# Empty rows of the expert buckets: stored behind the counts instead of over the whole range in batch 0

## The chip, the cores and the metric

The kernel runs on one core of one Trainium2 chip, as one launch. The metric is the device time in microseconds (us), the median of several runs. Five engines work side by side, each in its own order: TensorE (PE, its weight loads PEld), VectorE (DVE), ScalarE (ACT), GpSimd (POOL) and SyncE (SP), which here issues most of the DMAs.

## The reference

A ReLU-squared attention without softmax is multiplied into u, and its result goes token by token through one of 16 experts. B = 8 batches of S = 1856 tokens, D = 256, z has 64 columns, an expert's hidden width is 1024:

```python
scores = (1.0 / S) * np.matmul(z, z.transpose(0, 2, 1))
attn = np.maximum(scores, 0.0) ** 2
x = (u * np.matmul(attn, v)).reshape(B * S, D)
g_idx = np.argmax(x @ w_group, axis=1)
...
e_idx = np.argmax(xg @ w_expert[g], axis=1)
...
h = np.maximum(xg[mask_e] @ w1[g, e], 0.0)
ye = h @ w2[g, e]
out[tok_idx] = combined[:, None] * ye
```

`combined` is the product of the two softmax weights of the chosen group and expert. Each of the 14848 tokens thus goes to exactly one of 16 experts, and how many an expert gets is known only when the router has run.

## The kernel before, in words

**Attention.** The 8 batches are cut into 4 chunks of queries (512, 512, 512 and 320 wide in batches 1 to 7, 512, 512, 416 and 416 in batch 0), and each chunk into 15 steps of 128 keys: 480 steps `s`, in step with which everything else is issued. `scores` runs six steps ahead of `attn_v`. Each factor is split in a high and a low part, and three products are added. The scores are symmetric, so some tiles are transposed by DVE (`put_mirror`), stored in DRAM (`sym`) and loaded again by `load_mirror` (tile `at`, L326) some steps before they are needed.

**Router.** At the end of a chunk (`chunk_end`) DVE makes `xT` = o * u (L429), ACT splits it (`xh`, L435) and writes planes of 16 bits (`pl`, L464); DMA transposes on SP's queue turn those planes into token rows (`rows`, L470) and the logits into `lgx` (L493). The generators of `route` then take small DVE steps, a few per attention step: the chosen expert, the place of each token in its bucket (`di`, from the running counts `base`), the weight. At the end POOL scatters the rows into the bucket with indirect DMAs (L642).

**Bucket.** `bucket` lies in DRAM and has a region of CAPB rows per expert, RW = 264 words (1056 B) a row: 256 of the token, its weight, its number and filling. The experts are then worked off in fixed numbers of rows, the capacities CAPS (1216 for the largest expert down to 832). A region's rows behind its tokens must therefore hold rows without effect: `padrow`, weight 0 and token number N or more, which the final scatter leaves out. Before the change `prefill` writes the first CMAX = 1280 rows of every region with `padrow`, in 32 stores of 640 rows, at steps 1 to 41 of batch 0 (list PFILL), and all scatters come later.

**Experts.** `sort_experts` runs on DVE twice: behind batch 6, when it fixes the two largest experts (NEARLY = 2) for an early start with their first FRZ = 512 rows each, and at the end with the final counts. It writes the experts in order of size to `eli`, and their regions to `rli`; SP reads both into registers (`regs`, L741 and L742). A block of up to 512 rows is then loaded by `load_x`: one DMA transpose (`xp`, L756) and a small load of weights and numbers (`meta`, L759); DVE joins it (`xf`, L770), ACT and DVE split it. `phase1` (L791 to L793) and `phase2_t` (L864) are the expert's two matmuls, ACT and DVE evacuate, `yr` (L877) turns the result back, and POOL scatters it into the output (L889). Expert weights (`raw_e`, L181 and L184) come 4 x 512 KB per expert. Blocks 0 and 1 belong to the two early experts and are worked in among the last steps of batch 7; blocks 2 and 3 are the rest of expert 0 (its place in the order, as everywhere below), 4 and 5 that of expert 1, and then each expert has two or three blocks.

**What sets the order.** In batches 1 to 7 PE, ACT and DVE run in the order in which the code issues them; outside of that a scheduler orders them by its own clock. SP's queue is ordered by the scheduler. SP works strictly in order: while one of its DMAs waits for a semaphore, everything behind it waits too. Its DMAs share eight completion counters. A DMA that touches `bucket` at an address known only at run time counts as touching all of it: it waits for the reads and writes of `bucket` that were issued before.

Two buffers matter below. The planes `pl` and the block loads `xp` share two buffers (`new_pl`), and `rows` has four (`new_rows`):

```python
    def new_pl(name):
        return sb("pl", [P, 2048], U16, 2, name)
```

Of the kernel before, what the change touches and what calls it, by code (L numbers as in the profile page):

```python
# [19 lines left out]
P = 128  # L20
CAPS = (1216, 1136, 1104, 1072, 1024, 1008, 992, 992, 960, 944, 928, 912, 896, 880, 848, 832)
OVT = 256
# [7 lines left out]
def tile_glu_attn_moe(  # L30
# [28 lines left out]
    assert all(sum(x) == S for x in QW)  # L59
    assert all(cv % 16 == 0 and cv >= 2 * P for cv in caps)  # L60
    RW = D + 8
    RU = 2 * RW
    CAPB = (N + 511) // 512 * 512 + 512
    CMAX = (max(caps) + P - 1) // P * P
    NROW = NE * CAPB
    NL = 20
    LP = 48
# [7 lines left out]
    POS = [KB.index(i) for i in range(NQ)]  # L75
    ATL = 7
    NT = 4
    NEARLY = 2
    PFILL = [1 + i for i in range(17)] + [18 + 5 * i // 3 for i in range(2 * NE - 17)]
    assert CMAX % (2 * P) == 0  # L80
    FRZ = min(512, min(caps[:NEARLY]))
    assert min(caps[:NEARLY]) > FRZ or len(set(caps)) == 1

# [5 lines left out]
    def sb(tag, shape, dt, bufs, name):  # L89
        return pool.tile(shape, dt, tag=tag, bufs=bufs, name=name)  # L90
# [28 lines left out]
    def bank(pl, tag, name):  # L119
        return pl.tile([P, 512], F32, tag=tag, name=name)  # L120

    bucket = tc.dram_tile([NROW + OVT, RW], I32, name="bucket")
    views = dram_disjoint_views(bucket, B * NQ * NT)

    padrow = cst("padrow", [P, RW], I32)
# [84 lines left out]
    def new_w():  # L210
        return {"h": [], "l": [], "2": []}
# [135 lines left out]
    def scores(s):  # L347
        b, c, i = steps[s]
        k = key(b, c, i)
        w = QW[b][c]  # L350
        for far in (ATL, 12):
            lb, lc, li = steps[min(s + far, NS - 1)]
            lk = key(lb, lc, li)
            if lk % KT == 0 and mirrored(lb, lc, lk) and ((lc, lk) == (3, 8) and lb < B - 1) == (far != ATL):
                load_mirror(lb, lk // KT, KB[lc])
        if mirrored(b, c, k):
            at = ats[(b, k // KT, KB[c])][:, k % KT]
            ah, al = new_z(f"ah_{s}")[:, 0:w], new_z(f"al_{s}")[:, 0:w]
            nc.scalar.copy(out=ah.rearrange("p (g x) -> p g x", x=32), in_=at)
            nc.vector.tensor_sub(  # L360
                out=al.rearrange("p (g x) -> p g x", x=32), in0=at, in1=f32(ah).rearrange("p (g x) -> p g x", x=32)
            )
            hl[s] = (ah, al)
            return
        z2h, z2l = bz[(b, k // 4)]
        ks = slice((k % 4) * P, (k % 4 + 1) * P)
        zm = zms[(b, c)][:, 0:w]
        ps = bank(ps_s, "s", f"sc_{s}")
        held = pin if s < LEAD + NK else same
        held(nc.tensor.matmul(ps[:, 0:w], z2h[:, ks], zm, start=True, stop=False))  # L370
        held(nc.tensor.matmul(ps[:, 0:w], z2l[:, ks], zm, start=False, stop=True))  # L371
        a = new_zraw(f"r_{s}")[:, 0:w]
        held = pin if s < NK else same
        held(nc.scalar.activation(out=a, in_=ps[:, 0:w], func=AF.Relu, scale=1.0 / S))  # L374
        ah = new_z(f"ah_{s}")[:, 0:w]
        mirror = MB[0] <= b < MB[1] and KB[c] < MC and k // KT < MC and c < POS[k // KT]
        if i in (ACT_TWICE[c] if MB[0] <= b < MB[1] else ()) and s >= NK:
            held(nc.scalar.activation(out=ah, in_=a, func=AF.Square))
            held(nc.scalar.activation(out=a, in_=a, func=AF.Square))
        else:  # L380
            held(nc.scalar.activation(out=a, in_=a, func=AF.Square))  # L381
            held(nc.vector.tensor_copy(out=ah, in_=a))  # L382
        if k < NKF:
            al = new_z(f"al_{s}")[:, 0:w]
            held(nc.vector.tensor_sub(out=al, in0=a, in1=f32(ah)))  # L385
        else:
            al = None
            nc.vector.tensor_sub(out=ah[TAIL:P, :], in0=a[TAIL:P, :], in1=f32(ah[TAIL:P, :]))
        if mirror:
            put_mirror(b, c, k, a)  # L390
        hl[s] = (ah, al)
# [27 lines left out]
    def chunk_end(s):  # L419
# [83 lines left out]
        defer(s + PL + 1, lambda: planes(1))  # L503
        defer(s + LG, logits)
        defer(s + LG + (1 if XO else 0), logits_out)
        wait = 5 if last else 12 if b == 0 and c < 2 else (17 if c == 1 and b < B - 1 else 15) if s + 1 < NS - NK else 8
        alone = b == B - 1 and c >= NQ - 2
        if c % 2 or alone:
            gens.append((max(s + wait, PFILL[-1] + 2), route(b, c // 2, (c % 2,) if alone else (0, 1))))
        if last_sort(b, c):  # L510
            gens.append((0, sort_experts()))
        if last:
# [18 lines left out]
    def route(b, half, hs):  # L531
# [102 lines left out]
        ew = t("ew", [NT8])  # L634
        nc.vector.tensor_reduce(out=ew, in_=sel, axis=AX.X, op=ALU.add)
        yield
        for h, (rows, nt, part) in enumerate(chunks):
            i0 = 4 * h
            nc.vector.tensor_mul(out=rows[:, 0:nt, D].bitcast(F32), in0=ew[:, i0:i0 + nt], in1=smv[:, i0:i0 + nt, 0])
            for i in range(nt):  # L640
                n = part if part and i == nt - 1 else P
                nc.gpsimd.indirect_dma_start(  # L642
                    out=views[(b * NQ + 2 * half + hs[h]) * NT + i],
                    out_offset=bass.IndirectOffsetOnAxis(ap=di[0:n, i0 + i:i0 + i + 1], axis=0),
                    in_=rows[0:n, i, :],
                    in_offset=None,
                )
            yield
# [4 lines left out]
    def sort_experts(final=False):  # L653
# [2 lines left out]


        sq = lambda name: sb("tm", [P, D], F32, 2, name)[:, 0:NE * NE].rearrange("p (a b) -> p a b", b=NE)
        key = cst("skey", [P, NE])
        nc.vector.tensor_sub(out=key, in0=base, in1=ebase)  # L660
        nc.vector.tensor_scalar(out=key, in0=key, scalar1=float(NE), scalar2=None, op0=ALU.mult)
# [31 lines left out]
        t2 = sq("t2")  # L693
        nc.vector.tensor_tensor(out=t2, in0=gt, in1=iota16.unsqueeze(2).to_broadcast([P, NE, NE]), op=ALU.mult)
        yield
        ef = cst("sef", [P, NE])
        nc.vector.tensor_reduce(out=ef, in_=t2.rearrange("p e j -> p j e"), axis=AX.X, op=ALU.add)
        yield
        nc.vector.tensor_copy(out=eli, in_=ef)
# [31 lines left out]
    NB = len(blocks)  # L731
    last_use = {j: max(i for i in range(NB) if blocks[i][0] == j) for j in range(NE)}
    is_sorted = []
    ereg = {}
    rreg = {}

# [164 lines left out]
        ocnt[0] += 1  # L901
        return oviews[ocnt[0] - 1]

    def prefill(i):
        r0, n = i // 2 * CAPB + i % 2 * (CMAX // 2), CMAX // 2
        ins = nc.sync.dma_start(
            bucket[r0:r0 + n, :].rearrange("(p t) w -> p t w", p=P),
            padrow.unsqueeze(1).to_broadcast([P, n // P, RW]),
        )
        tc.keep_in_program_order(ins)  # L910

    nc.vector.memset(warm, 0.0)
    nc.scalar.activation(out=warm, in_=warm, func=AF.Exp)
# [41 lines left out]
    for s in range(NS):  # L955
        b, c, k = steps[s]
        if s == NK:
            region.enter_context(tc.manual_schedule(engines={mybir.EngineType.PE, mybir.EngineType.Activation, mybir.EngineType.DVE}))
        if s == NS - NK:
            region.close()  # L960
        if s in (1, 4):
            pz.pop(0)()
        if s in (2, 6, 9):
            pv.pop(0)()
        if s == 8:
            make_router()
        for i in range(2 * NE):
            if PFILL[i] == s:
                prefill(i)
        nxt = s // NK + 1  # L970
        if k == 3 and nxt < B * NQ:
            load_ut(nxt // NQ, nxt % NQ)
        if b + 1 == B:
            for pc, load, cut in WPREP:
                if (c, k) == load:
                    wts.setdefault(0, new_w())
                    prep[pc] = load_w(regs(0)[0], wts[0], pc, "e0")
                if (c, k) == cut:
                    prep.pop(pc)()
        for what, pb, n in begin.get(s, ()):  # L980
            prep[(what, n)] = (prep_v if what == "v" else prep_z)(pb, n)
        for what, pb, n in split_at.get(s, ()):
            prep.pop((what, n))()
        if k == (5 if s < NK else 5) and nxt < B * NQ:
            prep_zm(nxt // NQ, nxt % NQ)
        if s == NS - NK - 6:
            load_rows(0)
        if s == NS - 6:
            load_rows(1)
        if s == NS - 12:  # L990
            xs.append(join_x(0, rows_b[0][0], blocks[0][2]))
        while ahead < min(NS, s + LEAD + 1, max(4, 3 + s + s // 2)):
            scores(ahead)
            ahead += 1
        attn_v(s)
        if k == NK - 1:
            chunk_end(s)
        run_deferred(s)
        run_gens(s, 2 if b + 1 < B else (3 if c < 3 else 5))
# [3 lines left out]
    def more_rows(i):  # L1003
        if not (deferred or gens):
            while late["loaded"] < min(NB, i + 2):
                load_rows(late["loaded"])
                late["loaded"] += 1

    def early(i):
        run_deferred(late["at"])  # L1010
# [132 lines left out]
    for i, (e, r0, n) in enumerate(blocks):  # L1143
# [10 lines left out]
        def mid(f):  # L1154
            if i < NEARLY:
                early(i)
            elif i > 2 * NEARLY and f % 2 == 0:
                next(planned, None)
            if i + 1 == NB and f > 3 and unsent:
                unsent.pop(0)()  # L1160
            if ld is not None and f in (3, 5):
                sp[(f - 3) // 2]()
# [28 lines left out]
    with tc.For_i(0, kreg) as iv:  # L1191
# [6 lines left out]
        for t in range(2):  # L1198
            nc.gpsimd.indirect_dma_start(
                out=bucket,  # L1200
                out_offset=bass.IndirectOffsetOnAxis(ap=ix[:, t:t + 1], axis=0),
                in_=padrow,
                in_offset=None,
                bounds_check=NROW + OVT - 1,
                oob_is_err=False,
# [43 lines left out]
```

## Time and profile before

| | |
|---|---|
| median of 3 runs | 1456.65 us (1456.34 to 1457.46) |
| the profiled execution's own time | 1457.97 us |
| its span, first to last instruction | 1456.3 us |
| granted clock of PE, mean | 0.997 |
| PE busy | 1438.4 us (99%) |
| DVE, ACT, POOL busy | 1135.6, 920.2, 286.5 us |
| DMA moved | 255.98 MB, 176 GB/s on the mean |
| stores of `padrow` | 32 of 660.0 KB |

How to read it: a row of a timeline has the start and the duration in us, the engine, the line of the kernel, the operation and its tiles, and in brackets how long the engine stood idle before it and what released it. SPq is SP's sequencer: the duration is that of issuing the DMA, not of the transfer. A row of the waits has the waiting engine and line, what it waited for, and us in total, times and the longest. A row of the stretches has the busy time of each engine with its number of instructions, then PE's granted clock, the mean share in which the DMA engines were busy, and GB/s. Matmuls are pipelined, so PE's busy time is not its peak. Batch 0 takes about the first 100 us, batch 7 ends at about 768 us, and the experts fill the time from about 760 us on.

### The profile page before, as it was taken

The numbers are of one execution on the slowest core, as the hardware profiler recorded it, in microseconds if no ns is written. First come the engines' busy times: TensorE is split into PE (matmuls) and PEld (weight loads), VectorE is DVE, ScalarE is ACT, GpSimd is POOL, SyncE is SP. The second block draws the span as 40 slices with busy tenths as digits, with TensorE's granted clock in tenths as the row PEclk, the third lists the DMA queues.
The fourth block names the chain that finished last, engine by engine and source line by source line (L and its number), as shares of the span: only waits on it lengthen the run. The fifth ranks groups of instructions, "written<-read, shape, count | busy, mean of one in ns | idle before, by whom it ended". The sixth has DMA issues, their size and how long they took to land. (4 is left out here: it accounts for less than half of the span.)

```text
span 1456.3 us, 22386 instructions
## 1 busy us (share of the span) xinstructions
PE 1438.4 (99%) x7113; PEld 1240.3 (85%) x7113; DVE 1135.6 (78%) x2338; ACT 920.2 (63%) x1613; POOL 286.5 (20%) x351
## 2 busy tenths in 40 slices
PE   9999999999999999999999999999999999999997
PEld 7898888888888888888788999888888888999986
DVE  7889999999998999989987576776566666666663
ACT  8887887788877878778675344444445444444442
POOL 0002022220222202221114222112211221122122
PEclk9999999999999999999999999999999999999998
DMA  9997979989799797997975464554533554555521
GB/s 290 327 258 210 231 192 259 213 229 217 185 262 217 213 225 188 261 218 176 233 176 150 95 179 86 121 141 123 143 90 96 141 128 130 133 127 133 131 59 44
DMA packets 410808, 255.98 MB, mean 176 GB/s; under 512 B 243791, under 2 KB 370131, under 8 KB 410688
## 3 DMA queue, kind: packets, MB, share of 16 engines
q1 hardware_dynamic: 398864, 223.51, 62.6%
q0 software_dynamic: 11744, 30.90, 6.8%
q8 instruction: 56, 0.92, 0.3%
q14 instruction: 64, 0.52, 0.1%
q10 hardware_dynamic: 80, 0.13, 0.0%
HBM read 108.29 MB, written 89.21 MB: 136 GB/s over the span
## 5 line engine op out<-in xcount | busy, mean ns | idle before, releaser
L407 PE MATMUL o<-ah,vl 128*128 128x512 f32 (+2 forms) x960 | 355.0, 370 | 1.7 <-DVE vl L294 1.5
L408 PE MATMUL o<-ah,vh 128*128 128x512 f32 (+2 forms) x960 | 354.7, 370 | 0.0
L410 PE MATMUL o<-al,vh 128*128 128x512 f32 (+2 forms) x896 | 329.4, 370 | 0.5 <-DVE al L360 0.5
L802 DVE SCALAR_TENSOR_TENSOR hl<-ph,hh 128x512 fp32r<-128x512 f32 (+12 forms) x288 | 173.2, 609 | 149.1 <-ACT hh L796 131.0
L864 PE MATMUL yT<-hh,w_e 128*128 128x512 f32 (+12 forms) x1120 | 269.4, 360 | 0.0
L796 ACT ACTIVATE hh<-ph 128x512 fp32r<-128x512 f32 (+12 forms) x288 | 152.4, 536 | 147.9 <-PE ph L793 140.3
L889 POOL DMA_INDIRECT out_dram<-y,meta x126 | 126.9, 1007 | 493.6 <-DVE y L887 463.1
L864 PEld LDWEIGHTS yT<-hh,w_e 128*128 128x128 f32 x1120 | 200.2, 188 | 25.0
L374 ACT ACTIVATE r<-sc 128x512 f32<-128x512 f32 (+2 forms) x312 | 177.8, 570 | 56.2 <-PE sc L371 38.6
L642 POOL DMA_INDIRECT bucket<-rows,di x121 | 137.5, 1137 | 367.8 <-issue 217.7
L407 PEld LDWEIGHTS o<-ah,vl 128*128 128x128 f32 x960 | 180.4, 188 | 32.1 <-DVE vl L294 2.1
L791 PE MATMUL ph<-xh_m,w1l_e 128*128 128x512 f32 (+12 forms) x576 | 206.8, 361 | 0.8 <-ACT xh_m L775 0.8
L792 PE MATMUL ph<-xh_m,w1h_e 128*128 128x512 f32 (+12 forms) x576 | 207.5, 361 | 0.0
L408 PEld LDWEIGHTS o<-ah,vh 128*128 128x128 f32 x960 | 180.3, 188 | 28.8
L793 PE MATMUL ph<-xl_m,w1h_e 128*128 128x512 f32 (+12 forms) x576 | 203.2, 360 | 0.0
L385 DVE TENSOR_TENSOR al<-r,ah 128x512 fp32r<-128x512 f32 (+2 forms) x280 | 188.0, 672 | 17.0
L410 PEld LDWEIGHTS o<-al,vh 128*128 128x128 f32 x896 | 168.0, 188 | 26.8 <-DVE al L360 0.8
L381 ACT ACTIVATE r<-r 128x512 f32<-128x512 f32 (+2 forms) x284 | 174.0, 613 | 9.0
L864 PE MATMUL yT<-hl,w_e 128*128 128x512 f32 (+12 forms) x560 | 159.2, 360 | 0.0
L867 ACT COPY yp<-yT 128x1024 uint16<-128x1024 uint16 (+2 forms) x70 | 59.2, 848 | 141.9 <-PE yT L864 78.4
L382 DVE CAST ah<-r 128x512 fp32r<-128x512 f32 (+2 forms) x284 | 117.4, 413 | 18.4 <-ACT r L381 13.1
L370 PE MATMUL sc<-zm,z2h 128*128 128x512 f32 (+2 forms) x312 | 120.5, 386 | 1.0 <-ACT r L374 0.6
(166 smaller groups left out, 1967.7 us busy)
## 6 DMA issues: line engine op xcount, KB each, us to landing
raw_e<-in_w_dram SPq DMA_DIRECT2D x64, 512.0 KB
sym<-mt SPq DMA_DIRECT2D x126, 256.0 KB
at<-sym SPq DMA_DIRECT2D x84, 256.0 KB
bucket<-padrow SPq DMA_DIRECT2D x32, 660.0 KB
at<-sym SPq DMA_DIRECT2D x84, 160.0 KB
vr<-in_v_dram SPq DMA_DIRECT2D x24, 512.0 KB
ut<-in_uT_dram SPq DMA_DIRECT2D x23, 512.0 KB
zr<-in_zT_dram SPq DMA_DIRECT2D x47, 128.0 KB
```

Source lines behind the costliest of these rows:

```text
L374: held(nc.scalar.activation(out=a, in_=ps[:, 0:w], func=AF.Relu, scale=1.0 / S))
L381: held(nc.scalar.activation(out=a, in_=a, func=AF.Square))
L385: held(nc.vector.tensor_sub(out=al, in0=a, in1=f32(ah)))
L407: held(nc.tensor.matmul(o, vl[:, dsl], ah, start=(i == 0), stop=False))
L408: held(nc.tensor.matmul(o, vh[:, dsl], ah, start=False, stop=end and al is None))
L410: held(nc.tensor.matmul(o, vh[:, dsl], al, start=False, stop=end))
L791: nc.tensor.matmul(o, wt["l"][d][:, fs], xh[:, d, 0:W], start=(d == 0), stop=False)
L792: nc.tensor.matmul(o, wt["h"][d][:, fs], xh[:, d, 0:W], start=False, stop=False)
L793: nc.tensor.matmul(o, wt["h"][d][:, fs], xl[:, d, 0:W], start=False, stop=(d == ND - 1))
L796: nc.scalar.activation(out=hh[:, 0:W], in_=o, func=AF.Relu)
L802: nc.vector.scalar_tensor_tensor(out=dst, in0=o[:, c0:c1], scalar=0.0, in1=f32(hh[:, c0:c1]), op0=ALU.max, op1=ALU.subtract)
L864: nc.tensor.matmul(o, wt["2"][f // 2][:, w0:w0 + P], hs[f][q // 2][:, 0:n], start=((f, q) == (0, 0)), stop=((f, q) == (NF - 1, 2)))
```

## The change

The prefill goes. Instead the rows behind an expert's tokens are stored once the counts are known, and as many as its capacity. `sort_experts` keeps a copy of the counts (`ends`), SP loads an expert's end into a register, and `pad` stores `padrow` from there. Behind batch 6's sort there are three such stores: 512 rows for expert 0, 512 for expert 1, and another 768 for expert 0. Behind the final counts there is one for each of the experts 1 to 15, of 640 to 1152 rows, ahead of the load of its first block with final counts. A bucket row has 258 words (1032 B) instead of 264. Some small edits come with it: the last mirror loads are issued 11 steps ahead and not 12, the first two chunks of batch 0 are routed as late as those of other batches, the planning of the overflow loop (`plan`) starts at block 9 instead of 5, and `sef` takes the buffer of `srank`.

```diff
+    BW = D + 2
-    CAPB = (N + 511) // 512 * 512 + 512
+    CAPB = N + (max(caps) + P - 1) // P * P
-    PFILL = [1 + i for i in range(17)] + [18 + 5 * i // 3 for i in range(2 * NE - 17)]
-    bucket = tc.dram_tile([NROW + OVT, RW], I32, name="bucket")
+    bucket = tc.dram_tile([NROW + OVT, BW], I32, name="bucket")
-        for far in (ATL, 12):
+        for far in (ATL, 11):
-        wait = 5 if last else 12 if b == 0 and c < 2 else (17 if c == 1 and b < B - 1 else 15) if s + 1 < NS - NK else 8
+        wait = 5 if last else (17 if c == 1 and b < B - 1 else 15) if s + 1 < NS - NK else 8
-                in_=rows[0:n, i, :],
+                in_=rows[0:n, i, 0:BW],
+        ends.append(cst("ends", [P, NE], I32))
+        nc.vector.tensor_copy(out=ends[-1], in_=base)
-    def prefill(i):
-        r0, n = i // 2 * CAPB + i % 2 * (CMAX // 2), CMAX // 2
-        ins = nc.sync.dma_start(
-            bucket[r0:r0 + n, :].rearrange("(p t) w -> p t w", p=P),
-            padrow.unsqueeze(1).to_broadcast([P, n // P, RW]),
-        )
-        tc.keep_in_program_order(ins)
+    def pad(j, n, off=0):
+        if (j, off) in padded:
+            return
+        padded.add((j, off))
+        e = regs(j)[0]
+        r0 = nc.sync.value_load(ends[-1][0:1, ds(e, 1)], min_val=0, max_val=(NE - 1) * CAPB + N)
+        n = (n + P - 1) // P * P
+        nc.sync.dma_start(
+            bucket[ds(r0 + max(off, 0), n), :].rearrange("(p t) w -> p t w", p=P),
+            padrow[:, 0:BW].unsqueeze(1).to_broadcast([P, n // P, BW]),
+        )
+    def pad_for(i):
+        if i < NB:
+            j = blocks[i][0]
+            pad(j, caps[j] - FRZ if j < NEARLY else caps[j], FRZ if j == 0 else -1 if j < NEARLY else 0)
...
+                    if pc == WPREP[0][0]:
+                        pad(0, FRZ)
...
+        if s == NS - NK - 4:
+            pad(1, FRZ)
+        if s == NS - NK + 0:
+            pad(0, caps[0] - FRZ, FRZ)
...
             while late["loaded"] < min(NB, i + 2):
+                pad_for(late["loaded"])
                 load_rows(late["loaded"])
                 late["loaded"] += 1
+            if late["loaded"] >= 2 * NEARLY:
+                pad_for(late["loaded"] + 0)
...
-            elif i > 2 * NEARLY and f % 2 == 0:
+            elif i > 4 * NEARLY and f % 2 == 0:
```

Where the stores stand is seen in SP's queue. The first of three places is the head of batch 7, right behind the loads of the registers for expert 0 (`eli`, `rli`; ISA rows are address arithmetic). Before:

```order
L742 TENSOR_LOAD rli_108
L742 ISA x2
L741 TENSOR_LOAD eli_107
L741 ISA x2
L326 DMA at_7_1_3_9523<-sym_7_1_3_9117 32x10x128 x4
L184 ISA
L184 DMA raw_e0_2_9447<-in_w2_dram 128x4x256
```

And now:

```order
L745 TENSOR_LOAD rli_108
L745 ISA x2
L915 ISA
L915 TENSOR_LOAD ends_9276
L915 ISA x2
L917 ISA
L917 DMA bucket_69<-padrow_70 512x1x258
L325 DMA at_7_1_3_9503<-sym_7_1_3_9085 32x10x128 x4
```

A load of expert 0's end and the first store have moved in ahead of the mirror loads for batch 7's last chunk. Further on in the same queue stands the load of block 0 (`xp_0`), with the logits, rows and mirror loads of batch 7 behind it. Before:

```order
L756 DMA_TRANSPOSE xp_0_9545<-bucket_69 128x4x512
L493 DMA_TRANSPOSE lgx_7_0_9020<-lgp_7_1_9365 128x8x48
L470 DMA_TRANSPOSE rows_7_1_9362<-pl_7_1_9364 128x4x128 x4
L326 DMA at_7_2_3_9604<-sym_7_2_3_9243 32x10x128 x4
L184 ISA
L184 DMA raw_e0_3_9658<-in_w2_dram 128x4x256
L759 ISA
L759 DMA meta_1_9818<-bucket_69 128x4x2
```

And now:

```order
L759 DMA_TRANSPOSE xp_0_9525<-bucket_69 128x4x512
L492 DMA_TRANSPOSE lgx_7_0_8988<-lgp_7_1_9335 128x8x48
L917 ISA
L917 DMA bucket_69<-padrow_70 512x1x258
L469 DMA_TRANSPOSE rows_7_1_9332<-pl_7_1_9334 128x4x128 x4
L325 DMA at_7_2_3_9612<-sym_7_2_3_9211 32x10x128 x4
L917 ISA
L917 DMA bucket_69<-padrow_70 768x1x258
L183 ISA
L183 DMA raw_e0_3_9666<-in_w2_dram 128x4x256
L762 ISA
L762 DMA meta_1_9818<-bucket_69 128x4x2
```

The second store stands between the load of block 0 and the four `rows` transposes of batch 7's second chunk, and the third between the mirror loads and the last weights of expert 0. The second store's wait list names the load `xp_0`, and that of `meta_1` the third store. The third place is expert 2, the first one whose region is stored as a whole, at the load of its first block (`xp_6`). Before:

```order
L756 DMA_TRANSPOSE xp_6_11048<-bucket_69 128x4x512
L181 ISA
L181 DMA raw_e2_0_10756<-in_w1_dram 128x1024
L181 ISA
L181 DMA raw_e2_1_10758<-in_w1_dram 128x1024
```

And now, where the expert's four weight loads are already ahead of it:

```order
L880 DMA_TRANSPOSE yr_3_10675<-yp_3_10674 128x4x128 x3
L917 ISA
L917 DMA bucket_69<-padrow_70 1152x1x258
L745 TENSOR_LOAD rli_108
L745 ISA x2
L915 ISA
L915 TENSOR_LOAD ends_10273
L915 ISA x2
...
L759 ISA
L759 DMA_TRANSPOSE xp_6_11065<-bucket_69 128x4x512
```

The load has moved from ahead of the weights to behind them, behind the turned results of block 3 and behind the store, with eight register loads between the two. On PE, ACT and DVE nothing moves between the head of batch 7 and the final sort but the cast that copies `base` to `ends`.

## Prediction before the run

> **What bounds the kernel now.** I read the page first, then the waits of TensorE (PE), then the stretches by engine.
>
> ```profile
> PE 1438.4 (99%) x7113; PEld 1240.3 (85%) x7113; DVE 1135.6 (78%) x2338; ACT 920.2 (63%) x1613; POOL 286.5 (20%) x351
> ```
>
> PE is busy for 1438.4 of 1456.3 us, and the change takes no matmul away. So it can only move what PE waits. These are its waits, longest first: us in total, times, longest.
>
> ```profile
> PE o L407 <- DVE vl L294: 1.5, 1, 1.5
> ...
> PE pk L605 <- ACT lgp L490: 1.0, 1, 1.0
> PE pl L483 <- DVE xl L440: 0.9, 1, 0.9
> PE ph L791 <- ACT xh_m L775: 0.8, 2, 0.5
> PE sc L370 <- ACT r L374: 0.6, 1, 0.6
> PE o L410 <- DVE al L360: 0.5, 1, 0.5
> ```
>
> All of them together are under 8 us; the rest of PE's idle time is the ends of the span. The pace of the matmuls is no reserve either. The stretches give us, busy time of PE, PEld, DVE, ACT and POOL with their counts, granted clock, DMA share and GB/s:
>
> ```profile
> 0.00:20.00 20.00, 16.79 (x99) 13.58 (x100) 14.29 (x27) 15.62 (x28) 2.69 (x33) 1.00 0.85 245
> ...
> 40.00:60.00 20.00, 20.00 (x90) 16.44 (x89) 16.13 (x30) 16.65 (x27) 0.00 (x0) 1.00 1.09 357
> ...
> 240.00:260.00 20.00, 20.00 (x91) 16.06 (x90) 19.02 (x45) 17.64 (x30) 0.00 (x0) 1.00 1.10 252
> ...
> 1440.00:1460.00 20.00, 5.84 (x32) 4.66 (x30) 2.68 (x7) 1.68 (x4) 6.04 (x6) 0.74 0.11 39
> ```
>
> With the prefill running (40 to 60) PE does 90 matmuls in 20 us, without it (240 to 260) 91. The 32 stores do not slow PE down. An edit that starts from a PE with so few waits has little to win and can lose wherever a wait is new.
>
> **Batch 0: the prefill goes.** Its stores, by their line (ns of one issue, least, median, most):
>
> ```profile
> L906 SPq DMA_DIRECT2D bucket<-padrow x32: 580/1546/2325, 13.2 to 96.8; - x32
> ```
>
> One PE wait lies in their time, at 98.5 us. It goes back to a late transpose of batch 0's logits, which stood among these stores on SP's queue:
>
> ```profile
> 89.84 0.69 DVE L547 COPY lgf<-lgx 128x640 uint16<-128x640 uint16 x1 [1.95 <-DMA lgx<-lgp]
> 92.41 1.04 ACT L435 CAST xh<-xT 128x416 fp32r<-128x416 f32 x2 [1.52 <-DVE xT L429]
> ...
> 99.13 0.46 PE L370 MATMUL sc<-zm,z2h 128*128 128x416 f32 x1 [0.61 <-ACT r L374]
> ```
>
> DVE stood 1.95 us, then ACT 1.52, then PE 0.61. Now nothing stands ahead of that transpose and its route starts five steps later (a wait of 17 instead of 12). I count the 0.6 as won; it lies between 0 and 0.6, since no other PE wait falls in that time.
>
> **The head of batch 7.** This is where the change adds waits. SP's queue there, before:
>
> ```profile
> 734.63 1.84 SPq L326 DMA_DIRECT2D at<-sym  x4
> 736.69 0.43 SPq L184 DMA_DIRECT2D raw_e<-in_w_dram  x1
> ...
> 739.81 5.20 SPq L756 DMA_TRANSPOSE xp<-bucket  x1
> 745.12 1.19 SPq L493 DMA_TRANSPOSE lgx<-lgp  x1
> 746.41 5.15 SPq L470 DMA_TRANSPOSE rows<-pl  x4
> 751.66 2.03 SPq L326 DMA_DIRECT2D at<-sym  x4
> ...
> 760.74 1.80 SPq L493 DMA_TRANSPOSE lgx<-lgp  x1
> ```
>
> The first store stands ahead of the mirror loads at 734.63. It overwrites rows of the bucket, so it waits until batch 6's scatters have landed. When that is, POOL shows: its last scatter, and the iota that reuses a row buffer of those scatters.
>
> ```profile
> 732.06 1.42 POOL L642 DMA_INDIRECT bucket<-rows,di  x1 [0.30 <-issue]
> ...
> 735.65 0.15 POOL L443 IOTA rows<- 128x21 int32 x1 [1.89 <-issue]
> ```
>
> So the store issues at about 735.65; with the shortest issue, 0.58, the mirror loads come at 736.23 instead of 734.63, 1.6 later. Its 512 rows of 1032 B are 0.78 of a prefill store (640 rows of 1056 B). One of those took 1.55 us where they followed one another, 2.33 at most, so the bytes cost between nothing (in a gap of the queue) and 1.8. What stands behind on the same queue, three weight loads and `xp_0`, shifts by 1.6 to 3.4; I take 2.2. The three extra register loads ahead of `xp_0` are hidden, since its issue of 5.20 us is a queue that is full.
>
> The second store is worse. Its address is known only at run time, so it must wait until `xp_0` has read the bucket; and behind it stand the four transposes of `rows_7_1`. How long such a read takes to land is seen at `xp_2`: issued until 803.98, and DVE released at 806.21, 2.2 later.
>
> ```profile
> 802.56 1.42 SPq L756 DMA_TRANSPOSE xp<-bucket  x1
> ...
> 806.21 1.07 DVE L770 COPY xf<-xp 128x1536 uint16<-128x1536 uint16 x1 [3.85 <-DMA xp<-bucket]
> ```
>
> `xp_0`'s issue ended at 745.01; shifted by 2.2 that is 747.2, landed 749.4, the store's issue done 750.0. The `rows` transposes began at 746.41, so they are 3.6 late. For the store's own bytes ahead of them I add 0.4 (between 0 and 1.8): 4.0.
>
> Who waits for them? ACT, then DVE, then PE, with nothing in between:
>
> ```profile
> 752.97 1.05 ACT L464 COPY pl<-xT 128x1024 uint16<-128x1024 uint16 x1 [1.31 <-DMA rows<-pl]
> 753.92 0.61 ACT L435 CAST xh<-xT 128x512 fp32r<-128x512 f32 x1
> ...
> 754.57 0.69 DVE L440 TENSOR_TENSOR xl<-xT,xh 128x512 fp32r<-128x512 f32 x1 [1.33 <-ACT xh L435]
> 755.18 0.53 DVE L547 COPY lgf<-lgx 128x640 uint16<-128x640 uint16 x1
> 755.60 1.35 DVE L770 COPY xf<-xp 128x2048 uint16<-128x2048 uint16 x1
> 756.83 0.32 DVE L552 TENSOR_TENSOR tm<-lgf 128x160 f32<-128x160 f32 x1
> 757.05 0.90 DVE L360 TENSOR_TENSOR al<-at,ah 128x320 fp32r<-128x320 f32 x2
> ...
> 757.61 0.56 PE L410 MATMUL o<-al,vh 128*128 128x320 f32 x2 [0.55 <-DVE al L360]
> ```
>
> ACT may not overwrite the plane buffer until the transposes have read it, and waits 1.31 for that already. Its copies lead to DVE's `xl`, DVE runs without a gap to `al`, and PE waits 0.55 for `al`. The chain has no slack, and ACT's and DVE's order is the same in the changed program there. So PE loses what the transposes lose: **+4.0**, with no cover. Its least is 1.4 (`xp_0` lands at 747.2 as before, plus 0.58, against 746.41); its most is 6.6 (3.4 instead of 2.2 on the queue, and 1.8 for the store's bytes).
>
> Earlier in that stretch ACT also gets its first weight tile 2.2 later, but any PE wait from that lies inside the 4.0: the chain's end is the same.
>
> **The third store** (768 rows, 1.17 of a prefill store, 1.8 us) stands ahead of `meta_1`, which reads the bucket and waits for it to land: 0.58 plus 2.2 to 4.0. So `rows_7_2` and the logits' transpose at 760.74 come 2.8 to 4.6 later than the 4.0, with their landing at about 771 to 772.5. DVE reads them at
>
> ```profile
> 766.47 0.35 DVE L547 COPY lgf<-lgx 128x320 uint16<-128x320 uint16 x1
> ```
>
> and 4.0 later is 770.5. DVE then stands 0 to 2 us. PE is in block 0 there, with several PSUM banks ahead of it, so I take **+0.5** of 0 to 2.
>
> **The per-expert stores.** From expert 1 on, each stands ahead of the `xp` load of its expert, which waits for it to land. The tightest is expert 2's, 1152 rows (1.76 prefill stores, 2.7 us at that pace). `xp_6` moves from ahead of the weights to behind `yr_3` and this store:
>
> ```profile
> 838.39 1.77 SPq L756 DMA_TRANSPOSE xp<-bucket  x1
> ...
> 843.48 4.98 SPq L877 DMA_TRANSPOSE yr<-yp  x3
> ...
> 862.59 1.33 DVE L770 COPY xf<-xp 128x2048 uint16<-128x2048 uint16 x1
> ```
>
> `yr_3` ended at 848.46; plus 0.58, 2.7 and 2.2 for the store, 853.9; plus 1.77 and 2.2 for `xp_6`, 857.9, against its use at 862.59. The cover is 4.7 us, and I count **0**. Without that cover PE would lose microsecond for microsecond. Later experts have a block more of lead. The narrower rows make the scatters 2% smaller, with starts at other offsets:
>
> ```profile
> L642 POOL DMA_INDIRECT bucket<-rows,di x121 | 137.5, 1137 | 367.8 <-issue 217.7
> ```
>
> All but the last three run beside PE's work; for those, which gate `xp_2`, I take 0, between -0.1 and half of the 1.1 us that one takes. The few added DVE casts of 16 columns lie beside PE.
>
> **Sum.** -0.6 + 4.0 + 0.5 = +3.9 us. The profiled execution took 1457.97 us, its span 1456.30 and 1.67 around it; the median of the runs is 1456.65, 1.32 lower. On the median the forecast is 1456.65 + 3.9 = **1460.5 us**, 0.27% slower. A measurement of this kernel can tell about 0.2%, 2.9 us, from no change.
>
> **Rivals.**
> - *The chain catches up.* The stretch in which the first store would issue has some room on the DMA engines (share 0.65):
>
> ```profile
> 720.00:740.00 20.00, 19.12 (x84) 15.06 (x83) 19.29 (x48) 12.09 (x20) 7.82 (x9) 1.00 0.65 179
> ```
>
> If the first store's bytes slip into a gap of the queue, the second costs only its least, 1.4, and with the 0.6 won the sum is +0.8: 1457.5, no change. It decides where the second store ends its issue before 749.2, less than 2.8 behind 746.41. Against it: the 5.20 us of `xp_0`'s issue.
> - *The expert stores block SP.* If a store lands over 4.7 us later than I count, because the 2 MB of weights ahead of it are still under way, `xp_6` is late. At 4 us more than the cover the sum is +7.9: 1464.5. For it: the loads of eight registers stand there too.
> - *The early relief is larger.* The place would be batch 0 and the loads of batch 1: with 32 stores gone, PE would have to win over 2.9 us net, so more than the chain loses. PE's waits before 100 us are 0.6 plus those of the first 10 us, ahead of the first store at 13.2. It would need the chain at its least and 4.3 us won that no row shows: 1453.5.
> - *The clock falls.* PE's longest wait, 1.5 us, lies in the first stretch shown, whose clock is 1.00. After the last matmul the clock falls: in the last stretch PE is busy 5.84 us, and a mean of 0.74 over 20 us is 5.2 us of pulses missing. If it falls to half, that is 10.4 of the 14.2 idle us, so it fell 3.8 us after PE stopped. Should the new stall reach 3.8 us in one piece, and the clock need as long to come back, half of it is lost besides, +1.9: 1462.4. Against it: the stall comes in pieces, at two logits matmuls and then at `al`. [...]
>
> **How the numbers follow.** Forecast, +2.9 to +6.6: 0.50. The chain catches up: 0.28. Expert stores: 0.11. Clock: 0.07. Early relief: 0.04. Slower by over 0.2% is 0.50 + 0.11 + 0.07 = 0.68, within 0.28, faster 0.04. The range runs from 1456.8 (under it the early relief and the lowest part of the first rival) to 1465.0 (over it half of the expert stores' case and little else). The forecast's own range is 1459.6 to 1463.3.
>
> **What would show it.** Right: SP's second store near 749 to 751, `rows` transposes 3 to 5 us late, ACT's `pl` copy waiting about 5 instead of 1.31 for `rows<-pl`, and new PE waits of 3 to 5 us in sum by 763, on `xh`, `xl` or `al`; no PE wait near 98; `xp_6` landed before its `xf`. Wrong: PE without new waits between 735 and 765, or PE waits on `xh_m` in the expert blocks that are longer than the 0.8 of before.

## The result and the profile after

The changed kernel took 1471.66 us (median of 4: 1464.35, 1474.33, 1469.76, 1473.56) against 1456.77 us before; the ratio is 1.0091 [1.0077, 1.0105]. The forecast was 1460.5, between 1456.8 and 1465.0. The direction was right, the loss of 15 us is four times the one forecast. The profiled execution is the fastest of the four (1464.35, span 1462.5); the other three ran at a mean clock of 0.996 where it ran at 0.999.

The waits of TensorE after: us in total, times, longest.

```profile
PE pl L481 <- ACT xh L434: 1.7, 1, 1.7
...
PE yT L867 <- ACT hh L799: 1.3, 1, 1.3
...
PE o L406 <- DVE ah L387: 1.3, 1, 1.3
...
PE o L409 <- DVE al L359: 0.8, 1, 0.8
```

The wait of `sc` on `r` near 98 is gone. New are `pl` on `xh`, `o` on `ah` and a longer `al`, all between 750 and 762. The `yT` on `hh` stands at 805.74: ACT made that `hh` only at 805.09, though the `ph` matmul behind which it stands is drawn until 800.79. No other profile has this wait there, and its cause is open. SP's queue near 740 shows the chain of the prediction:

```profile
733.61 0.69 SPq L917 DMA_DIRECT2D bucket<-padrow  x1
734.41 2.65 SPq L325 DMA_DIRECT2D at<-sym  x4
...
739.55 0.38 SPq L762 DMA_DIRECT2D meta<-bucket  x1
742.96 3.27 SPq L759 DMA_TRANSPOSE xp<-bucket  x1
746.35 1.19 SPq L492 DMA_TRANSPOSE lgx<-lgp  x1
748.60 0.63 SPq L917 DMA_DIRECT2D bucket<-padrow  x1
749.33 5.90 SPq L469 DMA_TRANSPOSE rows<-pl  x4
...
757.58 0.57 SPq L917 DMA_DIRECT2D bucket<-padrow  x1
...
764.50 0.40 SPq L762 DMA_DIRECT2D meta<-bucket  x1
```

TensorE is 1.2 us ahead of the kernel before at this point, so `rows` at 749.33 instead of 746.41 is 4.1 late; the forecast said 4.0. Its parts differ: three of the four register loads between `meta` and `xp` are new and were counted as hidden; the four take 3.0 us, the one before took 0.7, and the issue of `xp_0` is 1.9 shorter in return. ACT and TensorE answer along the chain foreseen, with one wait more, from the first weight tile (ACT stood 2.49 us for it before). ACT's `pl` copy then waited 2.44 us and not about 5, since ACT, held up by that weight tile, came to it 3.5 us late itself:

```profile
743.70 1.14 ACT L199 CAST w_e<-raw_e 128x512 fp32r<-128x512 f32 x2 [6.25 <-DMA raw_e<-in_w_dram]
...
756.45 1.04 ACT L463 COPY pl<-xT 128x1024 uint16<-128x1024 uint16 x1 [2.44 <-DMA rows<-pl]
```
```profile
752.69 0.42 PE L406 MATMUL o<-ah,vl 128*128 128x320 f32 x1 [1.26 <-DVE ah L387]
...
758.07 0.43 PE L481 MATMUL pl<-xh,whl 128*48 128x512 f32 x1 [1.73 <-ACT xh L434]
...
761.05 0.56 PE L409 MATMUL o<-al,vh 128*128 128x320 f32 x2 [0.82 <-DVE al L359]
```

That explains under 5 us. To find the rest, the two traces were laid side by side: both have 7113 matmuls in nearly the same order, so the start of the n-th in one minus its start in the other tells how far a kernel has fallen behind. The table gives what each profiled execution lost to the profiled kernel before in each stretch (places by the time of the kernel before, us; the experiments are below).

| profile | 20 to 130 | 130 to 740 | 740 to 772 | 772 to 838 | 838 to 870 | 870 to 1440 |
|---|---|---|---|---|---|---|
| changed kernel, first profile | -1.4 | 0.1 | 4.8 | 1.1 | -0.6 | 3.0 |
| e1, the same again | -1.4 | 1.6 | 7.9 | 0.6 | 1.5 | 3.0 |
| e2, place back | -1.4 | 2.8 | 7.9 | -0.2 | 3.9 | -0.1 |
| e3, before, place moved | 0.2 | 1.5 | 0.3 | -0.5 | -0.2 | 2.9 |
| e4, width back | -1.4 | 1.7 | 5.3 | -0.5 | 2.6 | 3.0 |
| e5, late stores, prefill | 22.3 | -2.1 | -0.5 | -0.5 | 2.8 | 3.0 |
| e6, early stores, prefill | 22.0 | -2.0 | 4.7 | -0.5 | -0.8 | 3.0 |
| e7, stores on POOL | -1.4 | -2.1 | 3.8 | 0.0 | -0.8 | 3.0 |
| e8, early stores together | -1.4 | -2.1 | 11.0 | -0.5 | 1.9 | 3.0 |
| e10, before, register loads | -0.1 | 4.2 | -0.1 | -0.6 | 4.0 | 0.0 |
| e11, POOL, place, width | -1.4 | 0.7 | 3.7 | 3.5 | -0.8 | -0.1 |

Three places lose: the head of batch 7, the stretch near 850 and the expert phase from 870 on, where no wait is shown at all. What falls between 130 and 740 is put down to chance and not to the change: single stalls of under 1 us at changing places, which e10, the kernel before as far as 740, has too (0.77, 0.98 and 0.60). e5 to e8 ran on a chip where the kernel before itself took 1453.97 us, 2.8 to 4.5 us less than elsewhere.

### The profile page after: what moved, and what is told of

Same layout as the page of the kernel before. It is cut to its first block, busy times and chain, and to the rows that moved or that the text cites. A ratio compares the mean times of both kernels' runs of the same rounds, so it can differ in the third digit from the quotient of the medians.

```text
span 1462.5 us, 22473 instructions
## 1 busy us (share of the span) xinstructions
PE 1442.4 (99%) x7113; PEld 1240.1 (85%) x7113; DVE 1137.1 (78%) x2340; ACT 922.8 (63%) x1613; POOL 286.2 (20%) x351
## 5 line engine op out<-in xcount | busy, mean ns | idle before, releaser
L796 PEld LDWEIGHTS ph<-xl_m,w1h_e 128*128 128x128 f32 x576 | 108.2, 188 | 14.5
```

Of the source, the lines that this page charges most:

```text
L796: nc.tensor.matmul(o, wt["h"][d][:, fs], xl[:, d, 0:W], start=False, stop=(d == ND - 1))
```

## The experiments

Each is compared with executions of the kernel before on the same chip.

**Is the pace in the expert phase a matter of place, stores or row width? (e1 to e4.)** The three mirror buffers, which also hold `w1h` of the experts, lie 320 B lower after the change: the route is asked for later, so its tiles `sm`, `sel` and `ew` are allocated behind them. The theories were this place, the traffic of the stores, and the narrower rows.

> The changed kernel once more, nothing edited. Its four executions so far spread over 10 us (1464.35 to 1474.33), the profiled one being the fastest, while the kernel before spread over 1.1 us. If the spread belongs to the kernel, these runs lie in 1464 to 1475 again; and a profile of a slower execution shows where its further 5 to 10 us are (new waits on the xp loads would speak for the stores, a lower pace of the matmuls without waits for something that slows TensorE's operands). If it was chance, they lie within 1.5 us of one another.

Measured: 1470.42 us (1468.43 to 1471.78), ratio 1.008 [1.0066, 1.0094]. The loss is the kernel's own; these five executions spread over 3.4 us.

```
e2 (changed kernel), in load_mirror:
+ rt_.n = getattr(rt_, "n", None) or [rt_(*x, "spare") for x in (("sm", [40]), ("sel", [8, 4]), ("ew", [8]))]
```


> The changed kernel with the three tiles sm, sel and ew allocated ahead of the mirror buffers, so that those (which hold w1h of the experts too) lie at 204224 as before, not at 203904. No instruction moves. In the profiled runs the 128x512 matmuls of ph take 233.3 ns in the changed kernel and mostly 228.9 before. Placement theory: ph goes back to about 228.9 ns, and the kernel is at least 3 us faster than e1_again, up to 10 if the slower executions come from the same. Stores theory (the pace falls because of the stores' traffic in the expert phase): ph stays at 233 ns and the time equals e1_again within 2 us.

Measured: 1469.11 us, ratio 1.007 [1.0054, 1.0085]. The 3 us that were expected against e1 did not come: it was 1.3. By the trace the place counts all the same: from 870 on e2 loses -0.1 instead of 3.0, while near 850 its profile loses 2.4 more than that of e1.

```
e3 (kernel before), in route:
- sm = t("sm", [NG])
+ rt_.n = getattr(rt_, "n", None) or [new_at(f"spare{i}") for i in range(3)]; sm = t("sm", [NG])
```


> The kernel before with the mirror buffers allocated ahead of sm, sel and ew, so that they lie at 203904 as in the changed kernel. No instruction moves and no store. Placement theory: ph at 233 ns and 3 to 10 us slower than before, with a wider spread. Stores theory: equal to before within 1 us, ph at 228.9.

Measured: 1460.89 us, ratio 1.0014 [1.0005, 1.0023]: about 2 us, less than expected, with 2.9 in the trace. The same block of 48 `ph` matmuls, its first and its last, in the kernel before and then in e3 (start, us):

```profile
1134.81 0.39 PE L791 MATMUL ph<-xh_m,w1l_e 128*128 128x512 f32 x1
...
1145.57 0.39 PE L793 MATMUL ph<-xl_m,w1h_e 128*128 128x512 f32 x1
```
```profile
1137.00 0.40 PE L791 MATMUL ph<-xh_m,w1l_e 128*128 128x512 f32 x1
...
1147.96 0.40 PE L793 MATMUL ph<-xl_m,w1h_e 128*128 128x512 f32 x1
```

10.76 us against 10.96 for 47 steps: 4.3 ns more for each, with no wait and the clock at 1.00. The `yT` matmuls, which read no tile that was moved, start every 227 ns in both. The place theory holds for this stretch, and for no other: e2 keeps the rest of the loss.

```
e4 (changed kernel): BW = D + 8; CAPB = (N + 511) // 512 * 512 + 512; max_val of the load of ends 1024 lower
```


> The changed kernel with rows of 264 words again (and the experts' regions shortened to the 15360 rows of before, so that the bucket fits). Row width theory (rows of 1032 B start at odd offsets, so xp reads and scatters are slower): xp issues and scatters get shorter and several us come back, up to all of the 10 that the forecast missed. Placement and stores theories: within 2 us of e1_again.

Measured: 1469.33 us, ratio 1.008 [1.0064, 1.0095], as e1. By the time the row width is no part of the loss. By the traces it could be some 1 us of the head at most: 5.3 less the 1.7 that 3.41 us at half clock cost is 3.6, against 4.8 in the first profile.

**What is behind 4.8 against 7.9 at the head? (The clock.)** Stretches of the first profile after, then of e1, whose waits there are the same within 0.5 us. The third number from the right is the granted clock, the one ahead of it in brackets POOL's count.

```profile
760.00:765.00 5.00, 4.18 (x24) 3.64 (x23) 4.04 (x10) 2.26 (x4) 0.00 (x0) 1.00 0.95 226
765.00:770.00 5.00, 5.00 (x26) 4.32 (x26) 4.23 (x15) 3.29 (x8) 0.00 (x0) 1.00 0.41 80
```
```profile
760.00:765.00 5.00, 4.01 (x16) 3.13 (x16) 5.00 (x10) 3.97 (x7) 0.00 (x0) 0.70 1.12 235
765.00:770.00 5.00, 5.00 (x19) 4.32 (x18) 3.18 (x9) 2.09 (x5) 0.00 (x0) 0.62 0.42 97
```

In e1 the clock is at half from 761.95 for 6.83 us: 19 matmuls in 5 us instead of 26. e2 has 6.83 us of it there and 3.41 at 858, e4 3.41 at 761, the first profile none: the spread of the executions. This was the prediction's rival with a chance of 0.07, with a stall of 3.8 us as its condition. Whether the stall alone brings it was tried on the kernel before, with one stall put in (e13 to e16; N spare copies, and TensorE's products of that block in the order written):

```
e13 to e16 (kernel before), in phase1, ahead of hh; N = 12, 15, 18, 24:
+ for _ in range(N if (name, f) == (12, NF - 1) else 0): nc.scalar.copy(out=spare, in_=o[:, 0:224])
```


> The kernel before with one stall of TensorE put into the expert phase and nothing else: ahead of the last hh of the 13th block ACT makes 12 spare copies of 128x224, and TensorE takes that block's products in the order written. TensorE needs this hh 14 matmuls (3.2 us) later; at about 0.33 us a copy, as for a 128x256 hh, it waits about 1.4 us, in one piece. Theory (the granted clock halves for one or two spans of 3.41 us behind a span in which TensorE stood some 1.4 us or more, whatever it stood for): at this length in some executions at most; 1 to 3 us slower than before. [...]

> As e13_stall_12 with 15 copies: a stall of about 2.4 us. Theory: the half clock follows in most executions, for 3.4 to 6.8 us, so 1.7 to 3.4 more than the stall: 4 to 6 us slower than before. [...]

> As e13_stall_12 with 18 copies: a stall of about 3.4 us. Theory and rival alike: the half clock follows; 5 to 7 us slower than before. That the stall alone costs (no half clock): 3.4.

> As e13_stall_12 with 24 copies: a stall of about 5.3 us. The half clock follows for 6.8 us at least: 8 to 9 us slower than before. If it lasts as long as the stall lasted, more than that: 10.

| | stall shown | half clock | lost in the trace | time, ratio |
|---|---|---|---|---|
| e13 | 1.93 | 3.41 | 3.8 | 1460.85, 1.002 [1.0011, 1.0029] |
| e14 | 3.06 | 3.41 | 4.9 | 1462.99, 1.0042 [1.0029, 1.0055] |
| e15 | 4.19 | 6.83 | 6.7 | 1464.02, 1.0045 [1.0032, 1.0058] |
| e16 | 6.46 | 6.83 | 8.8 | 1467.44, 1.007 [1.0057, 1.0083] |

The stalls came out longer than planned, since a copy took 0.375 us (4.50 for 12). e14's stall, and the eight matmuls behind it:

```profile
979.78 0.73 PE L865 MATMUL yT<-hh,w_e 128*128 128x512 f32 x2 [3.06 <-ACT hh L797]
980.35 3.18 PE L865 MATMUL yT<-hl,w_e 128*128 128x512 f32 x8
...
983.33 1.06 PE L865 MATMUL yT<-hh,w_e 128*128 128x512 f32 x2
```

Eight matmuls take 2.98 us, 0.37 each, instead of 0.23. One stall of 1.93 us is enough (e13), without any store, and the four stalls cost 1.8 to 2.5 us more than themselves: behind them TensorE works at half for 3.4 to 4.9 us. With e13 the prediction's condition of 3.8 us falls. In the 3.41 us ahead of each fall behind 740, the profiles of e1, e2, e4, e5, e8 and e13 to e16 show TensorE standing for 1.4 to 3.4 us in all. A single wait of 1.73 in the first profile after (ended at 758.07), and 1.87 within 3.41 us in batch 0 of e6 (up to 120.8), had no fall behind them. So the bound is open.

**Which stores cost near 850? (e5, e6, e10.)**

```
e5 (changed kernel): the 32 prefill stores of before kept, rows of 258; the three stores of batch 7 left out
e6 (changed kernel): the same prefill kept; the stores per expert left out
```


> The changed kernel with the prefill of batch 0 kept (32 stores of 640 rows of 1032 B) and without the three stores at the head of batch 7; the stores per expert stay. The mirror buffers lie at 203904 as in the changed kernel. Theory (the loss is the chain at the head of batch 7 and the half clock behind it, plus the place of w1h, plus SP's register loads at the second expert): no PE wait and no half clock near 750 to 770, 3 us from the place, 1 to 3 us near 850, nothing won in batch 0: 4 to 6 us slower than before. Rival (the stores per expert carry most of it, by their traffic or by SP standing still): 10 us or more slower than before, spread over the expert phase.

> The changed kernel with the prefill of batch 0 kept, the three stores at the head of batch 7 kept, and none of the stores per expert. Mirror buffers at 203904. Theory: the head of batch 7 costs 4.7 us as in the first profile of the changed kernel, and up to 3.4 more where the clock halves; with 3 us from the place and no waits near 850: 8 to 11 us slower than before. Rival (the stores per expert carry most): 3 to 5 us slower than before.

Measured: 1482.33 us, ratio 1.0194 [1.018, 1.0208], and 1483.90 us, ratio 1.0206 [1.0192, 1.022]. Both expectations missed, by 22 us that fell in batch 0. From there on the table separates the two parts of the change: e5 loses nothing at the head and 2.8 near 850, e6 loses 4.7 at the head and nothing near 850. The 22 us are the prefill with rows of 1032 B, which neither kernel compared here has; the kernel before with narrow rows alone has it:

```
e9 (kernel before): bucket and every access to it with rows of D + 2 words
```


> The kernel before with rows of 258 words instead of 264 and nothing else. In e5_late_only and e6_early_only the matmuls of batch 0 fell 22 us behind, and their prefill's packets of 1032 B took 75 ns on average where those of 1056 B took 55 before. Theory (the narrow rows slow the prefill, and all loads queued among it): 19 to 23 us slower than before, all of it ahead of 130 us. Rival (something else in those two kernels cost it): under 3 us slower.

Measured: 1486.40 us, ratio 1.018 [1.0161, 1.0198]; 28 us, more than expected, nearly all ahead of 130 us. Some 5 us of that are the clock again: behind its long waits TensorE works for 10.7 us at half there, and for 10.0 and 9.3 in batch 0 of e5 and e6. SP's twelve stores in a row, before and in e9, and e9's longest wait:

```profile
17.68 22.73 SPq L906 DMA_DIRECT2D bucket<-padrow  x12
```
```profile
18.11 34.01 SPq L906 DMA_DIRECT2D bucket<-padrow  x12
```
```profile
69.31 0.71 PE L370 MATMUL sc<-zm,z2h 128*128 128x416 f32 x1 [12.67 <-ACT r L374]
```

Near 850, SP is late with the third expert's weights. Ahead of them stand expert 1's store, for whose landing `xp` waits, and the register loads: 44 in the expert phase instead of 29, some 0.6 us of SP each. In the first profile after, with the same queue, the weights were in time and nothing was lost there.

```
e10 (kernel before), in more_rows, once per expert from expert 1 on:
+ nc.sync.value_load(rli[0:1, ds(regs(j)[0], 1)], min_val=0, max_val=(NE - 1) * CAPB)
```


> The kernel before with one more register load on SP per expert from expert 1 on, where the changed kernel loads the address of its store; no store, no other change. Theory (SP is late near 850 because of the 15 loads more, some 0.6 us each, ahead of the weights of the third expert): a PE wait of 1 to 3 us near 850, with a half clock in some executions: 1 to 4 us slower than before. Rival (it is the stores' waits and bytes): equal to before within 0.5 us.

Measured: 1461.73 us, ratio 1.0022 [1.0011, 1.0033]. No store is in it. Its profile is of the slowest of twelve executions. SP issues the third expert's first weights 5.8 us later than the kernel before, and ACT waits for them 2.5 us longer; TensorE was 3.4 us behind there anyway. The kernel before, then e10:

```profile
840.83 0.56 SPq L181 DMA_DIRECT2D raw_e<-in_w_dram  x2
```
```profile
844.69 1.05 ACT L193 CAST w1h_e<-raw_e 128x1024 fp32r<-128x1024 f32 x1 [2.10 <-DMA raw_e<-in_w_dram]
```
```profile
846.64 0.99 SPq L181 DMA_DIRECT2D raw_e<-in_w_dram  x2
```
```profile
850.57 1.04 ACT L193 CAST w1h_e<-raw_e 128x1024 fp32r<-128x1024 f32 x1 [4.59 <-DMA raw_e<-in_w_dram]
```
```profile
851.95 0.98 PE L864 MATMUL yT<-hh,w_e 128*128 128x256 f32 x6 [2.25 <-ACT hh L796]
```
```profile
858.35 1.01 PE L867 MATMUL yT<-hh,w_e 128*128 128x256 f32 x3 [3.10 <-ACT hh L799]
```

So ACT waits and then TensorE, as in e2, whose wait is the last row. The register loads alone thus suffice for the place near 850; whether the stores would do it without them was not tried.

**Other ways to place the stores (e7, e8, e11, e12).**

```
e7 (changed kernel), in pad: nc.gpsimd.value_load and nc.gpsimd.dma_start instead of nc.sync
e8 (changed kernel): pad(1, FRZ) and pad(0, caps[0] - FRZ, FRZ) asked for right behind pad(0, FRZ)
```


> The changed kernel with all its stores, and the register loads of their addresses, issued by POOL instead of SP. Same bytes, same waits for landings; but nothing of SP's queue stands behind a store's wait any more. Theory (the queue behind the waiting store is what costs): the transposes of rows no longer wait for the reading of the bucket, the head of batch 7 costs under 2 us, the clock stays, and the weights near 850 are in time; with 3 us from the place and 1.2 won in batch 0: 2 to 4 us slower than before. Rival (the loads that wait for a store's landing cost it): 8 us or more slower than before, as with SP.

> The changed kernel with the second and the third store of batch 7 asked for where the first one stands, ahead of the first expert's loads, so that none of them waits for a bucket read. Theory: the wait for the landing of xp_0 goes, and 2 of the 3 us by which the transposes of rows were late; their 1280 rows more ahead of the weights cost 1 to 2 in turn: the head costs 2 to 4 us, with a half clock less often; in all 6 to 10 us slower than before. Rival (the store's wait for xp_0 does not matter, the traffic does): no better than the changed kernel, 12 us or more slower than before.

Measured: e7 1461.59 us, ratio 1.0055 [1.0041, 1.0069]; e8 1468.64 us, ratio 1.01 [1.0084, 1.0115]. POOL takes off the place near 850 (-0.8), but the head still costs 3.8, not under 2, and the time misses the 2 to 4 us expected. SP in e7:

```profile
732.39 1.55 SPq L180 DMA_DIRECT2D raw_e<-in_w_dram  x2
739.53 0.38 SPq L762 DMA_DIRECT2D meta<-bucket  x1
740.65 3.03 SPq L759 DMA_TRANSPOSE xp<-bucket  x1
...
745.07 5.76 SPq L469 DMA_TRANSPOSE rows<-pl  x4
```

SP stands 5.6 us in front of `meta`, which reads what the store writes. With the store on another queue, the wait moves to its reader. e8 missed its 6 to 10 us too, for no wait was saved in it: each store waits for the landing of the one before (issued at 730.73, 734.96 and 740.76), and `xp_0` for that of the third, until 750.26. So `rows` comes at 752.77, TensorE waits 2.21 and 2.62 us in one piece, and the clock falls twice.

```
e11: e7 with e2's place and e4's width      e12 (kernel before), in prefill: nc.gpsimd.dma_start
```


> e7_pool_queue (all stores of the changed kernel issued by POOL) with the mirror buffers back at 204224 and rows of 264 words. Theory: e7's 7.6 us over before shrink by the 2.9 of the place, and by up to 1 of the width: 3 to 5 us slower than before; faster than the changed kernel by 10. Rival (the terms do not add, because the half clock comes anyway): 6 us or more slower than before.

> The kernel before with its 32 prefill stores issued by POOL instead of SP. If the 1.2 to 1.4 us that the changed kernel wins in batch 0 come from SP's queue being free of the prefill, they are won here too, without a store elsewhere: 0.6 to 1.4 us faster than before. Rival (the bytes themselves or the making of descriptors on POOL hold something up): 0 to 5 us slower.

Measured: e11 1461.87 us, ratio 1.0025 [1.0016, 1.0035], as expected. That its terms add is not shown, for its profile loses 3.5 us between 772 and 838, in waits of 1.77 and 1.22 us that e7 has not. e12 1465.63 us, ratio 1.0051 [1.0039, 1.0063], a miss: POOL issues the stores from 2.6 us on, where SP began at 13.2, eight of them by 8 us, and TensorE is 8.4 us behind after 20 us. No version tried is faster than the kernel before.

## Why the forecast fell short, step by step

| step of the prediction | forecast | shown |
|---|---|---|
| batch 0 without the prefill | -0.6 | -1.4 |
| chain at the head of batch 7 | +4.0 | +4.8 |
| half clock behind it | a rival, +1.9, chance 0.07 | 0 to 3.4, in three of four profiles; none in e6 |
| third store | +0.5 | 0.2 at most |
| stores per expert | 0 | -0.6 to +3.9 |
| place of `w1h` | not in the sum | +3.0 |

- **The third store** cost next to nothing, though its landing was under-priced: `meta` behind it came at 764.50, 6.3 us after the issue, where 2.2 to 4.0 were counted. DVE stood 1.60 us for the logits, as foreseen, but TensorE fell back by only 0.2 us between 765 and 795.
- **Batch 0** was mis-sized. A wait of 0.61 in the list cost 0.9, since the matmul ahead of it is drawn 0.34 us long where the next would have started 0.19 after it; another 0.4 falls 4 us later, too short for the list. The route did not move by five steps but by three: the kernel before also held it back to two steps behind the last store of `prefill`, step 43, and now it starts at 46.
- **The head** was right in mechanism and nearly in size: first store behind batch 6's scatters, second behind the reading of `xp_0`, `rows` 4.1 late, `pl`, `xh` and `al` late in turn. That `rows` came out so close is in part luck, since 2.3 us of new register loads and an issue 1.9 shorter cancelled out. "Any PE wait from that lies inside the 4.0" was wrong: with the 1.26 of `ah` the head cost 4.8.
- **The clock** is the step that failed most. "It fell 3.8 us after PE stopped" put the missing pulses at the very end of a 20 us stretch of which the span fills 16.25, and made a condition that the stall in pieces could not meet. The same trace in finer stretches has the fall 1.95 us behind the last matmul's end at 1445.84, and e13 shows 1.93 in mid-kernel:

```profile
1445.84:1447.78 1.94, 0.00 (x0) 0.00 (x0) 0.89 (x2) 0.84 (x2) 1.08 (x2) 1.00 0.19 68
1447.79:1456.25 8.46, 0.00 (x0) 0.00 (x0) 0.00 (x0) 0.00 (x0) 0.91 (x1) 0.50 0.04 14
```

- **The stores per expert** failed at "I count 0": the cover of `xp_6` was priced with `yr`, a store and its landing, but the register loads of that queue were left out of the sum (a rival names eight of them without a price). In the profile after, the store of 1152 rows was issued until 855.45 and `xp_6` at 862.70, where 4.9 us were counted; up to 862.0 SP was busy with register loads, so most of the 7.25 us are theirs and not the landing's. Nor was `xp_6` what TensorE waited for: where it lost time near 850, it stood behind ACT's casts of that expert's weights, a path that the prediction did not price.

```profile
854.85 0.60 SPq L917 DMA_DIRECT2D bucket<-padrow  x1
862.70 2.15 SPq L759 DMA_TRANSPOSE xp<-bucket  x1
```

The register loads of the stores' addresses, all of that profile (ns of one, least, median, most; the reckoning around each brings it to some 0.6 us):

```profile
L915 SPq TENSOR_LOAD <-ends x18: 4/276/882, 732.9 to 861.4; - x18
```

- **The place** was not looked for: the prediction took the matmuls' pace as given. The diff moves no tile by a line of its own; a later first use did.
- Three small sums are off and change nothing: by its own terms the landing behind the third store is 771.5 to 773.3, not 771 to 772.5; the first rival leaves out the third store's 0.5; and the early relief comes to 1453.75, not 1453.5.

The sum for e1: -1.4 + 1.6 + 7.9 + 0.6 + 1.5 + 3.0 = 13.2, against 12.2 between the two spans; the last 1.0 is in the first 20 us and behind the last matmul. The loss of 15 us in the first measurement is thus not accounted for in full. For its three slower executions there is no trace; that they hold half clocks as e1 does is argued from their clock of 0.996 and not shown. It can't be all: 0.996 leaves 5.9 us of 1472, 6.6 with the rounding, the end of the program included, and two of them took 9.2 and 10.0 us longer than the profiled one. At least 2.6 us of each stay open.

## What to carry to other kernels

Where TensorE has no slack, price a stall of 2 us in one piece at nearly twice its length (e13 lost 3.8 us for one of 1.93), and look for the half clock in the granted clock of each execution, not in the waits. Count what a queue's engine itself does: here each store at an address known only at run time brought a register load of some 0.6 us, ahead of everything behind it in SP's queue. After any change, compare the addresses of the tiles that the matmuls read: when a loop slows without a wait, the n-th matmul against the n-th matmul shows it.

## What the runs showed of the hardware

- The place of the buffers that hold `w1h` changed the pace of the matmuls that read them: 320 B further down, 128x512 `ph` matmuls started every 233.2 ns instead of 228.9 (e3 against before; e2 against e1 shows the same the other way round). What in the address does it is open.
- The stores of the prefill were much slower with rows of 1032 B than of 1056 B: packets of 75 to 78 ns on average (75 in e5 and e6) against 55 (before), twelve stores in a row in 34.01 us (e9) against 22.73 (before). Whether it is the length or the offset of each row was not separated.
- The granted clock fell to half for 3.41 or 6.83 us behind a single stall of 1.9 to 6.5 us (e13 to e16), and in some executions behind shorter ones in a row (e1, not the first profile after), so the head of batch 7 cost 7.9 us in one execution and 4.8 in another of the same kernel.
